# An expert with a single chunk of rows gets an arm of its own for its first product, with the rows stationary

## The chip, the cores and the metric

The kernel runs on one core of a Trainium2 chip. The metric is the device time of one execution in microseconds (us), taken from outside the profile; before the change its median over three runs is 671.97 us.

## The reference, cut to what matters

Three stages follow one another: local attention, a mixture of eight experts (each token goes to one of them), and a Fourier mixer with a channel MLP. The change lies in the second.

```python
def _moe_ref(x, w_gate, w_local, w1, w2):          # x 2 x 768 x 512, w1 8 x 512 x 1024, w2 8 x 1024 x 512
    logits = np.einsum('bsd,de->bse', x, w_gate)
    local_gate = 1.0 / (1.0 + np.exp(-np.einsum('bsd,de->bse', x, w_local).squeeze(-1)))
    for b in range(B):
        prev_e = -1
        for s in range(S):
            fresh_e = int(np.argmax(logits[b, s]))
            e = fresh_e if s == 0 or local_gate[b, s] < 0.5 else prev_e     # prev_e >= 0
            prev_e = e
            ...
            h = np.maximum(x[b, s] @ w1[e], 0.0)
            out[b, s] = p[e] * (h @ w2[e])
def reference(...):
    x = attention(q, k, v)
    x = _moe_ref(x, **moe)
    return _moe2_ref(x, **moe2)                    # FFT mixer, layer norm, channel MLP
```

How many tokens an expert has depends on the data. With the inputs of these runs experts 0 to 7 have 324, 177, 166, 172, 115, 206, 96 and 280 tokens.

## The kernel before

Routing writes for each expert a list of its tokens. `Moe.expert(e, n, more)` then works through one expert in chunks of 128 rows; `n` is its number of chunks, held in registers and known only at run time. Experts 0 to 6 take one path of the code and expert 7 (`LAST`) another. In expert 0 the first chunk has been dealt with earlier, so its chunks here are 1 and 2 (`at = 1`); in the others they are 0 and 1 (`at = 0`).

**First product.** `first256` (L1160) always multiplies two chunks, 256 rows, with blocks of w1 stationary: four groups of 24 matmuls of 128x256, since float32 accuracy is made of three matmuls (weight and row each split in a high and a low part). After each group ScalarE takes the relu into `hh` (L1163), and VectorE the low part `hl` (L1164). A chunk that has no tokens is multiplied all the same. **Third chunk.** `third()` follows in a branch (L1226). **Second product.** `second` (L1140) multiplies the first chunk into `y` with 24 matmuls of 128x512; a branch (L1249) does the same for the second chunk, into `more`. An engine that does not take a branch jumps over it.

`first128` (L1190) is the other form of the first product, for 128 rows: the rows are stationary, and w1 streams past in two halves of 12 matmuls of 128x512. Its result lies the wrong way round for the second product, so ScalarE copies each half out of PSUM into `hs` (L1195), TensorE transposes it in four matmuls (L1179), and relu and low part follow (L1181, L1182). The third chunk and expert 7 use it.

**What runs beside it.** `ring.take` yields small steps, and `step` places two of them between the groups of matmuls; all engines run their instructions in the order in which they were emitted. The steps cast the next expert's weights: ScalarE rounds a piece of 128x1024 to the high part (L1006), and VectorE subtracts for the low part (L1008). Eight units of kind "d" go between them: pieces of a mixing matrix, stored as words of two halves, that are decoded here and used after the experts. Such a unit is an absolute value on ScalarE (L1019), four steps on VectorE (L1028, L1030, L1032, L1034) and a store to HBM on GpSimd's queue (L974). Experts 0 and 3 have two d units, one during each product, expert 6 has none, and the others have one during the first product. Their tiles, named `dec`, come from a pool of two buffers, which `hs` in `first128` shares. `tokens(e + 1)` places the transposes of the next expert's two chunks (L1102, in PSUM tiles `xtp` of a pool of two) between the matmuls of `y`, and ScalarE and VectorE take their two parts (L1105, L1106). On GpSimd's queue stand also the gathers of rows (L1070) and the scatters of results (L1127).

The framework counts the semaphores. Behind a branch, a wait is set so that it holds whichever arm was taken; the shorter arm adds what it lacks to the counts.

Of the kernel before, what the change touches and what calls it, by code (L numbers as in the profile page):

```python
# [23 lines left out]
P = 128  # L24
# [12 lines left out]
LAST = E - 1  # L37
# [850 lines left out]
def rows(st, g):  # L888

    n = 2 if g % 4 < 2 else 4  # L890
    out = []
    for j in range(2):
        hi, lo = (t.rearrange("p (k n) -> p k n", k=n) for t in st.ring.get("e", g + j))
        out += [(hi[:, k], lo[:, k]) for k in range(n)]
    return out
# [142 lines left out]
class Moe:  # L1038
# [79 lines left out]
    def write(self, y, p, d, name="more", beside=None):  # L1118

        nc = self.tc.nc  # L1120
        ys = self.work.tile([P, DM], F32, name=name, bufs=2 if name == "ys" else 1)
        nc.scalar.activation(ys, y, AF.Copy, scale=p)
        self.scatter(ys, d, beside)
# [74 lines left out]
    def expert(self, e, n, more):  # L1198
        tc, ring = self.tc, self.st.ring
        pc, ent = self.pc[e % 2], self.ent[e % 3]  # L1200
        w1, w2 = rows(self.st, 4 * e), rows(self.st, 4 * e + 2)
        bg = Background()

        def chain(*gs):
            for g in gs:
                yield from g


        at = 0 if e else 1
        step = lambda: bg.step(2)  # L1210
        spare = self.ps_more, "more"

        def result(c, h, y, ys, *more):
            y = self.second(*h, w2, *y, *more)
            bg.drain()
            last = e == LAST and c == 1
            write = lambda: self.write(y, pc[:, c:c + 1], ent[:, c, 1:2], ys, "first" if last else None)
            if last:
                self.finish = write
            else:  # L1220
                write()

        def third():
            self.weight(e, (2,))

            with tc.If(n > 2):  # L1226
                for _ in self.turn(2, 0, self.place(e, 2)):
                    pass
                if e == LAST:
                    self.rest(more)  # L1230
                late = self.first128(w1, *self.more, spare, spare)
                result(2, self.more[1], spare, "more", lambda: None, late)

        first, then = ([ring.take(*u, follow=e < LAST) for u in units] for units in ring.plan[e])
        if e < LAST:
            bg.add(chain(*first))
            self.gathers(e + 1)
            if e + 2 < E:
                self.entries(e + 2)
            calls = iter(range(8))  # L1240
            self.first256(e, lambda: bg.step(2) if e or next(calls) > 1 else None)
            bg.drain()
            if e:
                third()
            bg.add(self.tokens(e + 1))
            bg.add(chain(*then))
            own = lambda c: [t[0][:, :, c * P:(c + 1) * P] for t in (self.hh, self.hl)]
            result(at, own(0), (self.ps_y, "y"), "ys", step)
            with tc.If(n > at + 1):  # L1249
                result(at + 1, own(1), spare, "more")  # L1250
            return

        for c in range(2):
            x, h = ([t[:, :, c * P:(c + 1) * P] for t in s] for s in ((self.xh[e % 2], self.xl[e % 2]), (self.hh[0], self.hl[0])))
            late = self.first128(w1, x, h, (self.ps_h, "h"), (self.ps_x, "xtp"), step, [x[:, :DM] for x in self.xg[:2]])
            if c == 0:
                third()
                bg.add(chain(*first))
            result(c, h, (self.ps_y, "y"), "ys", step, late)
            if c == 0:  # L1260
                self.fetch(0)
# [562 lines left out]
```

## Time and profile before

| | us |
|---|---|
| median of 3 runs (lowest, highest) | 671.97 (671.45, 672.93) |
| the profiled execution | 671.14 |
| its span, and what lies outside it | 669.4 and 1.74 |
| busy in the span: TensorE, VectorE, ScalarE, GpSimd | 643.4, 391.7, 272.1, 68.5 |
| experts 0 to 6, first to last matmul (146.18 to 301.59) | 155.4 |

The engines are named PE (TensorE matmul), PEld (its weight load), DVE (VectorE), ACT (ScalarE), POOL (GpSimd) and SP (SyncE, which issues loads). A name such as ACTq is the engine's own sequencer. [...] A matmul's listed duration overlaps with the next one's: how long a row of them takes is read from the starts. Idle time ahead of an instruction stands in brackets with what ended it. L12 is line 12 of the kernel.

### The profile page before, as it was taken

What the parts mean: (1) busy time and instruction counts of PE and PEld (TensorE: products, weight loads), DVE (VectorE), ACT (ScalarE), POOL (GpSimd) and SP (SyncE); (2) the same over time, 40 slices, a digit from 0 to 9 for tenths busy, and PEclk for the clock granted to TensorE, in tenths of its full rate; (3) what the DMA queues carried; (4) which work ended last, traced back from release to release, by engine and by line L of the source; (5) the groups of instructions that cost most, each with busy time, mean ns of one, the idle gap of its engine ahead of it and who ended that gap; (6) DMA issues with size and microseconds to landing.
All of it is one profiled execution on the core that took longest, in us unless ns stands there. A gap on an engine that the chain in (4) does not pass through costs nothing.

```text
span 669.4 us, 9817 instructions
## 1 busy us (share of the span) xinstructions
PE 643.4 (96%) x3606; PEld 530.6 (79%) x3607; DVE 391.7 (59%) x931; ACT 272.1 (41%) x478; POOL 68.5 (10%) x83
## 2 busy tenths in 40 slices
PE   9999998879999999999999999999999999999997
PEld 5888887559988998897857687877788888888885
DVE  4667777518968789762357977899451131254112
ACT  6657666118555756563423542542221121141110
POOL 0010112230331333120100000000000000000000
PEclk9999999779999999999988799999999999999999
DMA  8656433447998799763260133353010010100001
GB/s 303 249 182 145 110 128 103 142 133 280 330 378 298 245 336 343 289 253 139 68 265 18 64 126 126 125 190 125 1 64 0 1 63 1 64 0 1 0 1 63
DMA packets 26096, 96.21 MB, mean 144 GB/s; under 512 B 7764, under 2 KB 8916, under 8 KB 18096
## 3 DMA queue, kind: packets, MB, share of 16 engines
q1 hardware_dynamic: 20288, 81.19, 35.5%
q0 software_dynamic: 4736, 10.56, 4.4%
q10 hardware_dynamic: 1008, 3.65, 1.4%
q8 instruction: 35, 0.57, 0.4%
q14 instruction: 29, 0.24, 0.1%
HBM read 84.75 MB, written 14.88 MB: 149 GB/s over the span
## 4 chain that ended last, share of the span: by engine, by line
PE 42%; DVE 9%; ACT 2%; issue 1%; DVEq 0%; ACTq 0%
PE h L1634 17%; PE acc L1649 5%; PE acc L1650 5%; PE acc L1648 5%; DVE dec L1032 1%; DVE dec L1034 1%; PE acc L1455 1%; PE y L1140 1%; PE more L1190 1%; PE h L1190 1%; PE acc L1469 1%; PE more L1140 1%; DVE dec L1030 1%; PE f L1600 1%; DVE dec L1028 1%
## 5 line engine op out<-in xcount | busy, mean ns | idle before, releaser
L1639 DVE SCALAR_TENSOR_TENSOR hl<-h,hh 128x512 fp32r<-128x512 f32 x48 | 33.1, 689 | 120.4 <-ACT hh L1638 120.4
L1638 ACT ACTIVATE hh<-h 128x512 fp32r<-128x512 f32 x48 | 28.7, 597 | 156.4 <-PE h L1634 151.4
L1008 DVE TENSOR_TENSOR wide<-raws,wide 128x1024 fp32r<-128x1024 f32 (+2 forms) x46 | 50.4, 1110 | 26.1 <-ACT wide L1006 26.0
L174 ACT ACTIVATE t<-t,nm 128x256 f32<-128x256 f32 (+1 forms) x96 | 39.2, 479 | 29.4 <-DVE nm L166 29.4
L1006 ACT CAST wide<-raws 128x1024 fp32r<-128x1024 f32 (+2 forms) x46 | 43.1, 959 | 6.4 <-PE acc L1650 3.5
L197 PE MATMUL op<-vs,p 128*128 128x75 f32 x352 | 43.5, 277 | 2.1 <-PE tp L183 1.1
L197 PEld LDWEIGHTS op<-vs,p 128*128 128x128 f32 x352 | 42.1, 195 | 3.0 <-PE tp L183 2.0
L1634 PE MATMUL h<-un0h,wide 128*128 128x512 f32 (+1 forms) x136 | 42.8, 381 | 0.1
L166 DVE CUSTOM_DVE_ANT_0 t<-sp,bias 128x256 f32<-128x256 f32 (+1 forms) x96 | 32.8, 398 | 9.7 <-PE sp L157 7.3
L1649 PE MATMUL acc<-wide,hh 128*128 128x512 f32 x96 | 38.2, 398 | 0.0
L1648 PE MATMUL acc<-wide,hh 128*128 128x512 f32 x96 | 37.9, 394 | 0.0
L1650 PE MATMUL acc<-wide,hl 128*128 128x512 f32 x96 | 37.7, 393 | 0.0
L1634 PEld LDWEIGHTS h<-un0h,wide 128*128 128x128 f32 x136 | 25.0, 188 | 5.5 <-ACT un0h L1410 0.3
L1163 ACT ACTIVATE hh<-h 128x512 fp32r<-128x512 f32 x28 | 16.8, 599 | 30.2 <-PE h L1160 26.7
L1160 PE MATMUL h<-xh,wide 128*128 128x256 f32 x192 | 27.7, 280 | 0.1
L1070 POOL DMA_INDIRECT xg<-xs,ent x23 | 25.4, 1104 | 14.2 <-issue 6.7
L1634 PE MATMUL h<-un0l,wide 128*128 128x512 f32 (+1 forms) x68 | 25.9, 380 | 0.0
L183 PE MATMUL tp<-consts,t 128*128 128x128 f32 x176 | 25.3, 281 | 0.5 <-ACT p L189 0.4
L1164 DVE SCALAR_TENSOR_TENSOR hl<-h,hh 128x512 fp32r<-128x512 f32 x28 | 19.2, 685 | 10.8 <-ACT hh L1163 8.6
L1160 PEld LDWEIGHTS h<-xh,wide 128*128 128x128 f32 x192 | 24.9, 188 | 0.8 <-issue 0.5
L189 ACT COPY p<-tp 128x512 f32<-128x512 f32 (+1 forms) x48 | 25.1, 536 | 0.7 <-PE tp L183 0.6
L183 PEld LDWEIGHTS tp<-consts,t 128*128 128x128 f32 x176 | 19.3, 143 | 5.0 <-PE sp L157 1.0
(441 smaller groups left out, 1609.6 us busy)
## 6 DMA issues: line engine op xcount, KB each, us to landing
raws<-we SPq DMA_DIRECT2D x30, 1024.0 KB
raws<-wm SPq DMA_DIRECT2D x17, 1024.0 KB
raws<-wmf SPq DMA_DIRECT2D x7, 1024.0 KB
wmf<-dec POOLq DMA_DIRECT2D x8, 512.0 KB, 8.6
vs<-v SPq DMA_DIRECT2D x6, 600.0 KB
xs<-xrow SPq DMA_DIRECT2D x12, 260.0 KB
vt<-vT SPq DMA_DIRECT2D x6, 512.0 KB
raws<-kq SPq DMA_DIRECT2D x3, 1024.0 KB
```

Of the source, the lines that this page charges most:

```text
L166: V.tensor_tensor_reduce(out=u.t[:, x, :u.W], in0=u.sp[:, j, k, :u.W], in1=bias[:, 4 * u.g + x, u.b0:u.b0 + u.W], scale=-0.125, scalar=3.0 ...
L174: A.activation(u.t[:, x, :u.W], u.t[:, x, :u.W], AF.Exp, bias=u.nm[:, x:x + 1], scale=-1.0)
L183: T.transpose(u.tp[k][:, j, c], u.t[:, 2 * k + j, c * P:(c + 1) * P], st.ident)
L197: T.matmul(u.op[:, x], u.p[:, x, c], vs[:, ti % KS, u.h + x], start=c == 0, stop=c == len(tiles) - 1)
L1006: (first or nc.scalar.copy)(hi[:, cs], raw[:, cs])
L1008: (eng() if callable(eng) else eng or nc.vector).tensor_tensor(lo[:, cs], raw[:, cs], hi[:, cs].bitcast(F32), op=ALU.subtract)
L1160: T.matmul(ps[:, u], w[:, f], x[:, k], start=n == 0, stop=n == 11)
L1634: nc.tensor.matmul(ps[:, c], a[:, k], x[:, k, c], start=n == 0, stop=n == 11)
L1639: nc.vector.scalar_tensor_tensor(hl, ps, 0.0, hh.bitcast(F32), op0=ALU.max, op1=ALU.subtract)
L1648: T.matmul(acc[c], hh[:, cs], h2, start=first, stop=False)
L1649: T.matmul(acc[c], hh[:, cs], l2, start=False, stop=False)
L1650: T.matmul(acc[c], hl[:, cs], h2, start=False, stop=last)
```

## The change

For experts 0 to 6 the first product gets a branch on the expert's count. With more than one chunk the `If` arm holds what was there, `first256` with its background steps. With one chunk the `Else` arm runs `first128` on it, 24 matmuls of 128x512 and two groups of four transposes, with the same casts and decodes beside it. The gathers of the next expert and the entries of the one after it stay ahead of the branch. The lines behind the edit move down by 10: L1249 becomes L1259, and L1241 is the new branch.

```diff
-        first, then = ([ring.take(*u, follow=e < LAST) for u in units] for units in ring.plan[e])
+        takes = lambda n: [ring.take(*u, follow=e < LAST) for u in ring.plan[e][n]]
         if e < LAST:
-            bg.add(chain(*first))
             self.gathers(e + 1)
             if e + 2 < E:
                 self.entries(e + 2)
-            calls = iter(range(8))
-            self.first256(e, lambda: bg.step(2) if e or next(calls) > 1 else None)
-            bg.drain()
+            begun = dict(ring.begun)
+            s = e % 2
+            with tc.If(n > at + 1) as two:
+                bg.add(chain(*takes(0)))
+                calls = iter(range(8))
+                self.first256(e, lambda: bg.step(2) if e or next(calls) > 1 else None)
+                bg.drain()
+            with two.Else():
+
+                ring.begun = begun
+                bg.add(chain(*takes(0)))
+                x, h = ([t[:, :, :P] for t in ts] for ts in ((self.xh[s], self.xl[s]), (self.hh[0], self.hl[0])))
+                self.first128(w1, x, h, (self.ps_h, "h"), (self.ps_x, "xtp"), step)()
+                bg.drain()
             if e:
                 third()
             bg.add(self.tokens(e + 1))
-            bg.add(chain(*then))
+            bg.add(chain(*takes(1)))
             own = lambda c: [t[0][:, :, c * P:(c + 1) * P] for t in (self.hh, self.hl)]
             result(at, own(0), (self.ps_y, "y"), "ys", step)
@@
             if c == 0:
                 third()
-                bg.add(chain(*first))
+                bg.add(chain(*takes(0)))
             result(c, h, (self.ps_y, "y"), "ys", step, late)
```

Three places show how instructions and waits move. The first is TensorE at the start of expert 0's second product, before:

```order
L1140 MATMUL y_6533<-wide_103,hh256_6304 128x512 x2
L1102 MATMUL xtp_6537<-consts_66,xg0_6328 128x128 [waits DMASW0_49]
L1102 MATMUL xtp_6537<-consts_66,xg0_6328 128x128 x3
L1140 MATMUL y_6533<-wide_103,hh256_6304 128x512
L1140 MATMUL y_6533<-wide_103,hh256_6304 128x512 [waits Activation_49]
L1140 MATMUL y_6533<-wide_103,hh256_6304 128x512
L1102 MATMUL xtp_6549<-consts_66,xg1_6329 128x128 [waits DMASW1_49]
L1102 MATMUL xtp_6549<-consts_66,xg1_6329 128x128 x3
```

And after:

```order
L1140 MATMUL y_6605<-wide_103,hh256_6304 128x512 x2
L1102 MATMUL xtp_6609<-consts_66,xg0_6328 128x128 [waits DMASW0_49,DVE_49,PE_49]
L1102 MATMUL xtp_6609<-consts_66,xg0_6328 128x128 x3
L1140 MATMUL y_6605<-wide_103,hh256_6304 128x512 x3
L1102 MATMUL xtp_6621<-consts_66,xg1_6329 128x128 [waits DMASW1_49,DVE_49,PE_49]
L1102 MATMUL xtp_6621<-consts_66,xg1_6329 128x128 x3
```

Each of the two transposes of tokens waited for its gather alone; now they wait for VectorE too, since the `Else` arm uses the two `xtp` tiles: the first for the ninth VectorE instruction of the `If` arm, the second for its last. All of experts 0 to 6 have this.

The second place is ScalarE in expert 4, from the start of the first product to its end, before:

```order
L1006 CAST wide_103<-raws_63 128x1024 [waits DMAHW2_49,PE_49]
L1163 ACTIVATE hh256_6304<-h_7691 128x512 [waits DVE_49,PE_49]
L1006 CAST wide_103<-raws_63 128x1024
L1006 CAST wide_103<-raws_63 128x1024 [waits DMAHW3_49]
L1163 ACTIVATE hh256_6304<-h_7722 128x512 [waits DVE_49,PE_49]
L1006 CAST wide_103<-raws_63 128x1024
L1019 ACTIVATE dec_7780<-raws_63 128x1024 [waits DMAHW4_49,DMASW0_49,DVE_49]
L1163 ACTIVATE hh256_6304<-h_7754 128x512 [waits PE_49]
L1163 ACTIVATE hh256_6304<-h_7788 128x512 [waits DVE_49,PE_49]
```

And the `Else` arm, which takes its place for one chunk:

```order
L1006 CAST wide_103<-raws_63 128x1024 [waits DMAHW2_49,PE_49]
L1006 CAST wide_103<-raws_63 128x1024 [waits PE_49]
L1006 CAST wide_103<-raws_63 128x1024 [waits DMAHW3_49,PE_49]
L1006 CAST wide_103<-raws_63 128x1024 [waits PE_49]
L1195 COPY dec_8156<-h_8157 128x512 [waits PE_49,Activation_49]
L1019 ACTIVATE dec_8185<-raws_63 128x1024 [waits DMAHW4_49,DMASW2_49,DVE_49]
L1181 ACTIVATE hh256_6304<-xtp_8192 128x4x128 [waits PE_49]
L1195 COPY dec_8156<-h_8180 128x512 [waits PE_49]
L1181 ACTIVATE hh256_6304<-xtp_8210 128x4x128 [waits PE_49]
```

Four casts now stand ahead of the first copy of a half, and the absolute value of the d unit (L1019) stands between the two copies. It waits for DMASW2, which here is the store of expert 3's second d unit; before, it waited for DMASW0, the store of expert 3's first. TensorE's two groups of transposes in that arm each wait for the copy of their half:

```order
L1190 MATMUL h_8180<-sl5h_6295,xh0_6322 128x512
L1190 MATMUL h_8180<-sl5l_6296,xh0_6322 128x512
L1179 MATMUL xtp_8192<-consts_66,dec_8156 128x128 [waits Activation_49]
L1179 MATMUL xtp_8192<-consts_66,dec_8156 128x128 x3
L1190 MATMUL h_8180<-sl5h_6295,xh0_6322 128x512
L1190 MATMUL h_8180<-sl5l_6296,xh0_6322 128x512
L1190 MATMUL h_8180<-wide_103,xl0_6325 128x512 x2
L1190 MATMUL h_8180<-sl5h_6295,xl0_6325 128x512 x2
L1179 MATMUL xtp_8210<-consts_66,dec_8156 128x128 [waits DVE_49,Activation_49]
L1179 MATMUL xtp_8210<-consts_66,dec_8156 128x128 x3
```

The third place is ScalarE at the end of expert 3's second product, before:

```order
L1006 CAST sl1h_101<-raws_63 128x1024
L1019 ACTIVATE dec_7608<-raws_63 128x1024 [waits DMAHW1_49,DMASW1_49,Activation_49]
L1122 ACTIVATE ys_7625<-y_7566,pc1_6309 128x512 [waits DMASW4_49,DVE_49,PE_49]
L1249 REGISTER_ALU x2
L1249 COMPARE_AND_BRANCH
```

And after:

```order
L1006 CAST sl1h_101<-raws_63 128x1024
L1019 ACTIVATE dec_7926<-raws_63 128x1024 [waits DMASW0_49,DMAHW1_49,DVE_49,Activation_49]
L1122 ACTIVATE ys_7943<-y_7884,pc1_6309 128x512 [waits DMASW4_49,PE_49]
L1259 REGISTER_ALU x2
L1259 COMPARE_AND_BRANCH
```

Expert 3's second absolute value waited for DMASW1, the store of expert 2's d unit. It now waits for DMASW0, the store of expert 3's own first. In expert 0 the second absolute value likewise waits for the store of the first.

## Rows read from the trace of the kernel before

**Rows 1.** Windows of two experts: stretch, length, busy time (instructions) by engine, PEclk, DMA share, GB/s

```profile
241.50:259.79 18.29, 17.99 (x129) 16.40 (x128) 15.63 (x21) 12.99 (x17) 6.56 (x7) 1.00 0.88 295
283.00:301.59 18.59, 18.29 (x131) 16.63 (x130) 12.04 (x16) 11.81 (x16) 4.56 (x4) 1.00 0.68 262
```

**Rows 2.** Timeline of TensorE, experts 4 and 6: start, duration, engine, line, operation, count

```profile
241.50 0.63 PE L1160 MATMUL h<-xh,wide 128*128 128x256 f32 x4
...
252.47 0.39 PE L1160 MATMUL h<-xl,sl5h 128*128 128x256 f32 x2
253.01 0.47 PE L1140 MATMUL y<-sl0h,hh 128*128 128x512 f32 x1
...
294.81 0.93 PE L1140 MATMUL y<-wide,hh 128*128 128x512 f32 x3
```

**Rows 3.** Timeline of TensorE, expert 7, which uses the other form

```profile
301.59 1.16 PE L1190 MATMUL h<-wide,xh 128*128 128x512 f32 x4
...
305.85 0.60 PE L1179 MATMUL xtp<-consts,xg 128*128 128x128 f32 x4
306.21 0.48 PE L1190 MATMUL h<-sl5h,xh 128*128 128x512 f32 x1
```

**Rows 4.** Timeline of ScalarE, expert 7: the copy of a half

```profile
304.65 0.59 ACT L1195 COPY xg<-h 128x512 f32<-128x512 f32 x1 [2.49 <-PE h L1190]
```

**Rows 5.** Timeline of TensorE: the end of the jump over the unused half of the attention

```profile
139.25 1.02 PE L50 MATMUL more<-busy 128*128 128x512 bf16 x4 [1.07 <-issue]
```

**Rows 6.** Timeline of TensorE, then VectorE, in expert 0: second tokens; last step of the decode

```profile
161.25 0.60 PE L1102 MATMUL xtp<-consts,xg 128*128 128x128 f32 x4
162.71 1.23 DVE L1034 SCALAR_TENSOR_TENSOR dec<-raws,dec 128x1024 int32<-128x1024 int32 x1
```

**Rows 7.** Timelines: second tokens and last low part in expert 3, then in expert 5

```profile
231.49 0.60 PE L1102 MATMUL xtp<-consts,xg 128*128 128x128 f32 x4
231.01 0.69 DVE L1164 SCALAR_TENSOR_TENSOR hl<-h,hh 128x512 fp32r<-128x512 f32 x1
273.29 0.60 PE L1102 MATMUL xtp<-consts,xg 128*128 128x128 f32 x4
273.81 0.68 DVE L1164 SCALAR_TENSOR_TENSOR hl<-h,hh 128x512 fp32r<-128x512 f32 x1
```

**Rows 8.** Timeline of GpSimd: expert 3's two stores; landing of all eight, then the second

```profile
231.39 0.58 POOL L974 DMA_DIRECT2D wmf<-dec  x1 [6.61 <-DVE dec L1034]
...
242.01 0.56 POOL L974 DMA_DIRECT2D wmf<-dec  x1 [10.03 <-DVE dec L1034]
DMA to landing us min/median/max: 7.0/8.6/10.0
DMA to landing us min/median/max: 7.8/7.8/7.8
```

**Rows 9.** Timelines of ScalarE, then VectorE: experts 3 and 4, d unit and casts

```profile
234.99 1.16 ACT L1019 ACTIVATE dec<-raws 128x1024 f32<-128x1024 f32 x1
...
242.33 1.04 ACT L1006 CAST wide<-raws 128x1024 fp32r<-128x1024 f32 x1
...
244.99 1.99 ACT L1006 CAST wide<-raws 128x1024 fp32r<-128x1024 f32 x2
237.78 0.69 DVE L1028 TENSOR_SCALAR dec<-dec 128x1024 f32<-128x1024 f32 x1
...
240.49 1.22 DVE L1034 SCALAR_TENSOR_TENSOR dec<-raws,dec 128x1024 int32<-128x1024 int32 x1
```

**Rows 10.** Timeline of TensorE at two gaps, each with the window that follows (columns as in 1)

```profile
143.49 2.02 PE L1102 MATMUL xtp<-consts,xg 128*128 128x128 f32 x8 [3.21 <-issue]
143.60:150.10 6.50, 5.83 (x26) 5.21 (x27) 1.50 (x4) 1.17 (x2) 2.03 (x2) 0.50 0.64 232
370.22 0.44 PE L1455 MATMUL acc<-wide,sl0l 128*128 128x386 f32 x1 [1.54 <-DVE sl0l L1411]
372.50:378.50 6.00, 6.00 (x19) 4.21 (x19) 5.66 (x22) 1.06 (x2) 0.00 (x0) 0.50 0.12 16
```

## The prediction

> **What bounds the kernel now.** I read the windows of the experts first. From the first matmul of expert 4 to that of expert 5 lie 18.29 us, in which TensorE is busy for 17.99, at the full clock; expert 6 takes 18.59 with 18.29 busy [rows 1]. No other engine reaches 16 us there. So TensorE paces this stage, and a microsecond taken from or added to its row of instructions comes out at the end, as long as the others keep up. A window does not show how near the others are to not keeping up. For that I read the timelines, and the order of the changed program, for each wait that is new.
>
> **What the edit is meant to take away.** In expert 4 the 96 matmuls of the first product, one jump and the start of the second product take 253.01 - 241.50 = 11.51 us [rows 2]; in expert 6 294.81 - 283.00 = 11.81. Expert 7 runs the other form: 18 matmuls of 128x512 take 305.85 - 301.59 = 4.26, so 0.237 each, and four transposes 0.36 [rows 3]. A whole arm is then 24 x 0.237 + 2 x 0.36 = 6.4 us on TensorE. With two jumps the second product could start 7.0 us in, 4.5 to 4.8 us earlier, in two experts (4 and 6, with 115 and 96 tokens). That gross gain of some 9 us is not what I forecast, since the halves have to go through ScalarE, and since the new arm changes waits in all seven experts.
>
> **Jumps.** The one jump over an arm not taken that is in the first rows costs TensorE 253.01 - (252.47 + 2 x 0.117) = 0.31 [rows 2], where 0.117 is 11.2 us over 96 matmuls (11.51 less the jump). Each expert now makes one more. The far jump over the attention's unused half cost at most 1.07 [rows 5]. The new arms are small, so I take 0.31; the end of the range is 1.07, or 0.76 more for each jump.
>
> **Expert 0: +2.7.** The second transposes of tokens stood at 161.25. They now wait for the last VectorE instruction of the first product, which here is the last step of a d unit, ending at 162.71 + 1.23 = 163.94 [rows 6]. Queued behind them on TensorE is the rest of the second product. The jump lies within this wait: +2.7. The second absolute value here now waits for the store of the first d unit, issued 0.3 behind that same step, landing 7.0 to 10.0 later [rows 8]. Behind it on ScalarE stands only the result's scaling, behind its decode on VectorE a cast for expert 2 and then expert 1's first low part. I take 0, as the tokens' wait has already moved TensorE by 2.7; up to 3.0 if the store needs 10.0 instead of 7.0.
>
> **Experts 1, 2 and 3: +0.9.** The same wait is there for the last low part, which in expert 3 ends at 231.70, against transposes at 231.49 [rows 7]: 0.2, within the jump's 0.31. Expert 3 stands for the three: 3 x 0.3.
>
> **Expert 4: +4.75.** This is the large term, and its cause begins in expert 3. There the second absolute value, at 234.99 before [rows 9], now waits for expert 3's first store, issued at 231.39 and landing 8.6 later (the median) at 240.0 [rows 8]. It ends at 241.2; two scalings of 0.6 follow, and the casts of expert 4 begin at 242.35, where they did (242.33). But the decode on VectorE, which takes 240.49 + 1.22 - 237.78 = 3.93 [rows 9], now ends at 245.1 instead of 241.7. The second store goes out 0.3 later, at 245.4, and with its 7.8 [rows 8] lands at 253.2, which is 11.7 after expert 4's start. All further times count from there. GpSimd's scatters and the gathers for expert 5 stand behind that store and move with it, but their rows are wanted only at 15.
>
> ScalarE: the casts start at 0.85; four at 0.97 (two took 1.99, [rows 9]) end at 4.75, and the copy of the first half (0.59, [rows 4]) at 5.3. TensorE, with its 18 matmuls done at 0.31 + 4.26 = 4.6, waits until then, transposes to 5.7, and ends its last six matmuls at 7.1. Next in ScalarE's row is the absolute value, held for the store until 11.7. It ends at 12.9, the relu at 13.45, the copy of the second half at 14.0. TensorE stands still from 7.1 to 14.0, transposes until 14.35, jumps, and begins the second product at 14.65, against 11.51: +3.15. VectorE then owes two short steps of the decode (0.7 each), a low part (0.6), two long steps (1.25 each) and the last low part: 18.05. The second tokens would come six matmuls and four transposes behind 14.65, at 16.45, and wait 1.6 for it. Sum 3.15 + 1.6 = 4.75. With both stores at 7.0 the same working gives +2.3, with both at 10.0 +8.3.
>
> [...]
>
> **Expert 5: +0.75.** The last low part ends at 274.49, the transposes stood at 273.29 [rows 7]: +1.2. ScalarE's part of it may shrink, since expert 4 gives its loads more time; then the jump's 0.3 is left. I take the middle.
>
> **Expert 6: -3.4.** There is no d unit, so nothing stands between the two copies. Casts until 4.75 and the first copy until 5.3 as above, transposes to 5.7, six matmuls to 7.1, second copy to 7.7, transposes to 8.05, jump: 8.4 against 11.81. The last low part is done at about 9.3, ahead of the tokens.
>
> **The clock: +1.6.** [...] Expert 4's gap is 6.9 long. Half the clock for 6.4 us costs 3.2, of which the 1.6 that the tokens wait anyway are hidden. Bounds 0 and 3.2.
>
> **Sum.** 2.7 + 0.9 + 4.75 + 0.75 - 3.4 + 1.6 = +7.3. The profiled execution took 671.14 (span 669.4, 1.74 around it), so 678.4; the median of the runs is 0.83 higher than it: 679.3.
>
> **Rivals.**
> A, faster: the waits cost nothing, because stores land before they are asked for and VectorE is done in time. Then expert 0 to 3 and 5 pay a jump each (+1.55), and expert 4 gains like expert 6 (-3.4): 1.55 - 6.8 = -5.2, 666.7. It decides at a landing below 234.99 - 231.39 = 3.6 us, and needs the token wait to be no wait. Every landing listed speaks against it (7.0 at least), and so does the 163.94 of expert 0.
> B, no change: only the stores are fast. Expert 4 then starts its second product at 8.4 but its decode delays the tokens by 1.6, so -1.6; with 2.7 + 0.9 + 0.3 - 3.4 the sum is -1.1, 670.9.
> C, a second fall of the clock: expert 0's gap is at most 2.4 long (163.94 less 161.25 and a jump), if it falls in one piece. After 1.54 idle the clock was 0.50 for 6.0 us in a later stretch, which was lightly loaded before [rows 10]; here TensorE had been fully busy. If it falls, up to 3.2 more: 682.5.
> D, long jumps: 0.76 more in experts 0 to 3, 5 and 6 less what the waits hide (expert 0's): 5 x 0.76 = +3.8, 683.1.
> E, the arm is not taken: neither expert has one chunk. Then waits alone are left, 2.7 + 6 x 0.3 = +4.5, 676.5. The token counts speak against it.
>
> **How the numbers follow.** Forecast (with its own spread of +2.3 to +8.3 in expert 4) 0.55, C 0.17, D 0.10, E 0.03, A 0.08, B 0.07. The forecast's own range is 675 to 683; with C and D on one side, and B and A left out, the range is 674.5 to 685.5. A measurement of this kernel can tell about 0.2% from no change, 1.3 us. B stands for "same" with 0.07, A for "faster" with 0.08, the rest is slower: 0.85.
>
> **What would show it.** In the changed profile: no L1160 in experts 4 and 6, and L1190 in their place (else E); in expert 0, L1102 a second time at about 164 with VectorE as releaser; L1019 in expert 3 and expert 4 idle until a store lands; a gap of some 7 us on TensorE in expert 4 between L1190 and the second group of L1179, and 0.50 in the clock behind it; second product of expert 6 at 8.4 after its start. I am wrong if L1019 starts at once in expert 4 (B), if tokens do not wait (A), or if expert 4 loses over 8.3 (a store or a load that I have not seen).

## The result, and the profile after

The changed kernel takes 679.54 us (median of 20 runs, 673.11 to 685.6), against 672.39 for the kernel before in its 20 runs. The ratio, from which disturbed executions are left out, is 1.0094, with a 95% interval of 1.0075 to 1.0113: slower by about 0.9%, or 6.3 us. The span of the profiled execution is 676.6 us, against 669.4.

The windows of the changed kernel that answer to [rows 1], for expert 0, expert 4 and expert 6, each from its first matmul to the next expert's (columns as there; PEclk is the clock granted to TensorE, as a share of its full speed):

```profile
147.36:176.44 29.08, 26.59 (x152) 23.74 (x153) 19.17 (x26) 13.84 (x17) 3.62 (x4) 0.88 0.87 319
...
247.84:269.06 21.22, 15.24 (x65) 11.41 (x64) 16.75 (x21) 13.28 (x17) 7.29 (x7) 0.92 0.84 282
...
292.93:310.23 17.30, 13.87 (x65) 10.21 (x64) 11.48 (x15) 11.80 (x16) 5.52 (x4) 1.00 0.72 256
```

Experts 4 and 6 have 65 matmuls listed instead of some 130, so the new arm runs. TensorE has 2.8 us less to do in expert 4 than before, and expert 4 is 2.9 us longer: 6.0 of its 21.2 us are idle. Expert 6 has 4.1 less to do and is only 1.0 shorter (the window of expert 6 in [rows 1] begins 0.3 us early; from the first matmul at 283.30 TensorE was busy for 17.99).

The timeline of TensorE in expert 0 shows the second product and the two transposes of tokens, as in [rows 6]:

```profile
160.30 0.86 PE L1140 MATMUL y<-wide,hh 128*128 128x512 f32 x3
161.99 0.63 PE L1102 MATMUL xtp<-consts,xg 128*128 128x128 f32 x4 [0.83 <-issue]
...
164.98 1.08 PE L1102 MATMUL xtp<-consts,xg 128*128 128x128 f32 x4 [1.66 <-issue]
```

VectorE's last step of the decode starts at 163.66 there, takes 1.23, and the second transposes follow it:

```profile
163.66 1.23 DVE L1034 SCALAR_TENSOR_TENSOR dec<-raws,dec 128x1024 int32<-128x1024 int32 x1
```

They take 1.08, where the first took 0.63. The window from their start shows why, PEclk 0.50:

```profile
164.90:166.00 1.10, 1.02 (x5) 1.05 (x6) 1.10 (x2) 0.00 (x0) 0.58 (x1) 0.50 0.31 30
```

For experts 3 and 4 the timelines of GpSimd, ScalarE and TensorE belong together; they answer to [rows 8], [rows 9] and [rows 2]:

```profile
237.41 0.59 POOL L974 DMA_DIRECT2D wmf<-dec  x1 [6.62 <-DVE dec L1034]
249.93 0.56 POOL L974 DMA_DIRECT2D wmf<-dec  x1 [11.93 <-DVE dec L1034]
```

```profile
244.54 1.12 ACT L1019 ACTIVATE dec<-raws 128x1024 f32<-128x1024 f32 x1 [3.44 <-DMA wmf<-dec]
...
248.67 3.88 ACT L1006 CAST wide<-raws 128x1024 fp32r<-128x1024 f32 x4
252.46 0.57 ACT L1195 COPY dec<-h 128x512 f32<-128x512 f32 x1
257.32 1.12 ACT L1019 ACTIVATE dec<-raws 128x1024 f32<-128x1024 f32 x1 [4.29 <-issue]
```

```profile
253.09 0.66 PE L1179 MATMUL xtp<-consts,dec 128*128 128x128 f32 x4 [0.89 <-ACT dec L1195]
...
259.46 0.66 PE L1179 MATMUL xtp<-consts,dec 128*128 128x128 f32 x4 [4.32 <-ACT dec L1195]
260.26 0.76 PE L1140 MATMUL y<-sl0h,hh 128*128 128x512 f32 x1
...
263.73 0.60 PE L1102 MATMUL xtp<-consts,xg 128*128 128x128 f32 x4
```

This is the chain of the prediction. The first store goes out at 237.41, and the absolute value starts 7.1 us later. The second goes out at 249.93, and expert 4's absolute value starts 7.4 later. ScalarE stands between its two copies for 4.29 us and TensorE between its two groups of transposes for 4.32. The second product starts 12.42 us into expert 4 (11.51 before). For expert 4's absolute value the profile names no releaser ("issue"); that it is the store there too is shown by e2_rot below, in which that wait is gone.

In expert 6 the second product starts at 8.77 us instead of 11.51. Of these 2.74 us, 1.74 are lost at the second tokens, whose gather has not landed (they stand 12.41 us after the start, and 8.77 + 1.90 = 10.67 would have been possible):

```profile
301.70 0.94 PE L1140 MATMUL y<-wide,hh 128*128 128x512 f32 x3
...
305.34 0.63 PE L1102 MATMUL xtp<-consts,xg 128*128 128x128 f32 x4 [1.57 <-DMA xg<-xs,ent]
```

### The profile page after: what moved, and what is told of

Same layout as the page of the kernel before. It is cut to its first block, busy times and chain, and to the rows that moved or that the text cites. A ratio compares the mean times of both kernels' runs of the same rounds, so it can differ in the third digit from the quotient of the medians.

```text
span 676.6 us, 9698 instructions
## 1 busy us (share of the span) xinstructions
PE 638.1 (94%) x3478; PEld 520.2 (77%) x3479; DVE 389.3 (58%) x927; ACT 272.2 (40%) x478; POOL 69.7 (10%) x83
## 4 chain that ended last, share of the span: by engine, by line
PE 41%; DVE 9%; ACT 2%; issue 1%; DVEq 0%; ACTq 0%
PE h L1644 16%; PE acc L1659 5%; PE acc L1660 5%; PE acc L1658 5%; DVE dec L1032 1%; DVE dec L1034 1%; PE y L1140 1%; PE acc L1479 1%; PE acc L1465 1%; PE more L1190 1%; PE h L1190 1%; PE more L1140 1%; DVE dec L1030 1%; PE f L1610 1%; DVE dec L1028 1%
## 5 line engine op out<-in xcount | busy, mean ns | idle before, releaser
L1649 DVE SCALAR_TENSOR_TENSOR hl<-h,hh 128x512 fp32r<-128x512 f32 x48 | 33.0, 688 | 120.4 <-ACT hh L1648 120.4
L1648 ACT ACTIVATE hh<-h 128x512 fp32r<-128x512 f32 x48 | 28.7, 597 | 156.4 <-PE h L1644 151.4
L1070 POOL DMA_INDIRECT xg<-xs,ent x23 | 26.9, 1170 | 15.6 <-issue 6.8
L1019 ACT ACTIVATE dec<-raws 128x1024 f32<-128x1024 f32 x18 | 20.6, 1142 | 15.6 <-issue 9.4
L1160 PE MATMUL h<-xh,wide 128*128 128x256 f32 x160 | 22.7, 280 | 0.6 <-PEq L1259 0.6
L1034 DVE SCALAR_TENSOR_TENSOR dec<-raws,dec 128x1024 int32<-128x1024 int32 x18 | 22.1, 1225 | 0.6
L1644 PE MATMUL h<-un1h,wide 128*128 128x512 f32 x64 | 21.7, 400 | 0.7 <-ACT un1h L1420 0.7
```

The lines of the kernel that those rows point to most:

```text
L1034: V.scalar_tensor_tensor(t, lo, 29, t, op0=ALU.logical_shift_right, op1=ALU.bitwise_or)
L1644: nc.tensor.matmul(ps[:, c], a[:, k], x[:, k, c], start=n == 0, stop=n == 11)
L1649: nc.vector.scalar_tensor_tensor(hl, ps, 0.0, hh.bitcast(F32), op0=ALU.max, op1=ALU.subtract)
```

## The experiments

Each was run beside the kernel before, on the same chip as it. The table gives the lengths in us from the first matmul of an expert to that of the next, from the timelines of TensorE, the sum over experts 0 to 6, and the measured ratio to before. Without a stall expert 0 varies between 24.4 and 25.9 from one profile to another, as TensorE runs slower in the first part of it, for longer or shorter: PEclk is 0.50 for its first 4.1 us in the kernel before, and the matmuls of 128x256 start 0.21 us apart, instead of 0.12 behind that, for the first 2.8 us in e13_six_ent and the first 6.0 in e14_six_late; differences under 1.5 us in that column say nothing.

| kernel | 0 | 1 | 2 + 3 | 4 | 5 | 6 | sum | ratio (95% interval) |
|---|---|---|---|---|---|---|---|---|
| before | 25.05 | 23.43 | 46.84 | 18.29 | 23.51 | 18.29 | 155.41 | 1 |
| the change | 29.08 | 23.90 | 47.50 | 21.22 | 23.87 | 17.30 | 162.87 | 1.0094 (1.0075, 1.0113) |
| e1_never | 28.31 | 27.02 | 47.51 | 19.12 | 25.05 | 18.29 | 165.30 | 1.0109 (1.0075, 1.0143) |
| e2_rot | 28.27 | 23.75 | 47.49 | 16.86 | 25.94 | 15.62 | 157.93 | 1.0024 (0.9994, 1.0053) |
| e3_ps | 25.39 | 26.73 | 46.85 | 21.43 | 23.50 | 16.65 | 160.55 | 1.0075 (1.0046, 1.0105) |
| e4_both | 24.76 | 24.06 | 46.84 | 20.72 | 23.58 | 17.65 | 157.61 | 1.0022 (0.9996, 1.0048) |
| e5_no0 | 25.55 | 23.81 | 47.50 | 22.50 | 23.85 | 16.78 | 159.99 | 1.0049 (1.0014, 1.0084) |
| e8_six | 24.58 | 23.42 | 46.84 | 18.29 | 24.33 | 16.75 | 154.21 | 0.9973 (0.9955, 0.9992) |
| e9_free | 24.56 | 23.97 | 46.85 | 17.42 | 25.22 | 15.61 | 153.63 | 0.9979 (0.9953, 1.0006) |
| e10_free_q | 24.51 | 23.99 | 46.85 | 17.21 | 25.26 | 16.02 | 153.84 | 0.9963 (0.9937, 0.9989) |
| e11_free_ent | 25.32 | 32.03 | 46.83 | 24.24 | 23.50 | 15.60 | 167.52 | 1.0171 (1.0141, 1.0201) |
| e12_before_ent | 25.84 | 32.36 | 46.85 | 21.35 | 23.49 | 18.29 | 168.18 | 1.0163 (1.0118, 1.0208) |
| e13_six_ent | 24.43 | 31.58 | 46.80 | 18.81 | 23.50 | 15.60 | 160.72 | 1.0080 (1.0049, 1.0110) |
| e14_six_late | 25.87 | 23.42 | 46.84 | 18.29 | 24.07 | 15.66 | 154.15 | 0.9948 (0.9920, 0.9977) |

**The arm in the program, never taken (e1_never).**

```diff
-            with tc.If(n > at + 1) as two:
+            with tc.If(n > 0) as two:
```

> The new arm stands in the program, but its condition is changed so that no expert takes it: all of experts 0 to 6 run the old arm. Theory W (waits that the arm brings to everybody): expert 0 still loses its 4.0 us (tokens wait for VectorE, and the clock falls behind that), each of the other six pays a jump of 0.3, in all +5.8 us on the kernel before (ratio 1.0086, 1.006 to 1.010). Rival L (the loss is made inside the new arm, by its copies and transposes): only jumps are left, 7 x 0.31 = +2.2 us (1.003).

Measured 1.0109. The mere presence of the arm costs as much as the change, so the rival that lays the loss on the arm's own work falls. My own 5.8 us were too few: expert 1 takes 3.6 more, where I had put 0.3, and experts 4 and 5 together 2.4. At the end of expert 0 its second absolute value waits, by the order of the program for a store, as ScalarE's timeline shows, and with it the gathers of expert 2 come late in expert 1 (TensorE's timeline):

```profile
175.67 1.12 ACT L1019 ACTIVATE dec<-raws 128x1024 f32<-128x1024 f32 x1 [5.57 <-issue]
```

```profile
191.22 1.02 PE L1102 MATMUL xtp<-consts,xg 128*128 128x128 f32 x4 [1.03 <-DMA xg<-xs,ent]
```

**The two kinds of waits taken apart (e2_rot, e3_ps, e4_both).** In e2_rot the copied halves lie in the tile of the third chunk's rows, unused when there is one chunk, and both arms share one `dec` tile for a d unit:

```diff
-        t = self.work.tile([P, PW // 2], F32, name="dec")
+        t = self.pre.pop(r, None) if r in self.pre else self.work.tile([P, PW // 2], F32, name="dec")
@@
+            ds = [ring.at[u] for u in ring.plan[e][0] if u[0] == "d" and ring.at[u] not in begun]
+            held = {r: ring.work.tile([P, PW // 2], F32, name="dec") for r in ds}
+            ring.pre = dict(held)
@@
-                ring.begun = begun
+                ring.begun, ring.pre = begun, dict(held)
@@
-                self.first128(w1, x, h, (self.ps_h, "h"), (self.ps_x, "xtp"), step)()
+                own_hs = [self.xg[2 + e % 2][:, :DM]] * 2
+                self.first128(w1, x, h, (self.ps_h, "h"), (self.ps_x, "xtp"), step, own_hs)()
```

> The changed kernel with the store waits taken away: the copied halves go into an unused tile of gathered rows instead of the pool of decoded pieces, and both arms share one tile for a decoded piece, so that the buffers rotate as before the change. The tokens' wait for VectorE stays. Theory W: expert 4's second absolute value and copy start at once, expert 4 goes from +2.9 to about -1.6 (the second product 3 us earlier, the tokens 1.6 late), no clock fall there; expert 0 keeps +4.0, expert 6 its -1.3: +2.8 us on before (1.004, 1.002 to 1.006), 4.5 below the change. Rival L (ScalarE's order, not the store): nothing changes, +6 to +7 (1.009).

In e3_ps only the PSUM tiles of the transposes change:

```diff
-                self.first128(w1, x, h, (self.ps_h, "h"), (self.ps_x, "xtp"), step)()
+                self.first128(w1, x, h, (self.ps_h, "h"), spare, step)()
```

> The changed kernel with the transposes of the new arm in PSUM tiles of the other pool (that of the third and second chunks), so that the tokens wait for their gather alone as before. The store waits stay. Theory W: expert 0 goes from +4.0 to +0.3 and no half clock follows there; experts 1 to 3 and 5 pay a jump, expert 4 keeps about +2.5 and expert 6 -1.3: +2.7 us on before (1.004, 1.002 to 1.006). Rival L: no change against the changed kernel, 1.009.

e4_both has both edits.

> Both cures together: halves in an unused tile of gathered rows, one tile for a decoded piece in both arms, transposes in the other PSUM pool. Theory W: what is left is a jump in five experts (+1.5), and the gain of the arm in experts 4 and 6, -3.3 and -1.3 to -3.4 each: -3 to -5 us on before (ratio 0.992 to 0.996), faster than both. Rival L (the arm itself does not pay): no faster than before, 1.000 or above.

Each cure does in its own place what it should. With the store waits gone (e2_rot), expert 4 falls from 21.22 to 16.86 us, and expert 0 stays at 28.27. With the token waits gone (e3_ps), expert 0 falls to 25.39, experts 2 and 3 to what they were before, and expert 4 stays at 21.43. The totals follow the forecasts only in part. The 1.0024 of e2_rot lies within its range (1.002 to 1.006), though expert 5 is 2.4 longer and expert 6 shorter than that forecast had them; 1.0075 for e3_ps (range 1.002 to 1.006) and 1.0022 for both (0.992 to 0.996) lie outside. Three things are behind that.

First, the two waits cover each other in expert 0. When the tokens no longer wait, expert 0's store is late in relation to TensorE, and the 3 us come back in expert 1 of e3_ps, first on ScalarE, then on TensorE:

```profile
171.92 1.13 ACT L1019 ACTIVATE dec<-raws 128x1024 f32<-128x1024 f32 x1 [6.16 <-DMA wmf<-dec]
```

```profile
178.82 0.73 PE L1160 MATMUL h<-xh,wide 128*128 128x256 f32 x4 [1.00 <-DVE hl L1164]
...
187.64 0.63 PE L1102 MATMUL xtp<-consts,xg 128*128 128x128 f32 x4 [1.28 <-DMA xg<-xs,ent]
```

Experts 0 and 1 together take 48.48 before, 52.98 after the change, 52.02 and 52.12 with one cure, and 48.82 with both.

Second, in e2_rot an expert 4 that is 1.4 shorter than before is followed by an expert 5 that is 2.4 longer, as its casts wait for weights, and TensorE then for VectorE:

```profile
267.67 1.05 ACT L1006 CAST sl0h<-raws 128x1024 fp32r<-128x1024 f32 x1 [2.52 <-DMA raws<-we]
```

```profile
270.63 1.21 PE L1160 MATMUL h<-xh,wide 128*128 128x256 f32 x8 [0.84 <-DVE hl L1164]
```

Third, in e4_both expert 3's second absolute value still waits (4.66 us, until 242.01), for a store: the buffers rotate in another order there than in e2_rot, and the wait is gone in e9_free below, which takes the third chunk's halves out of that pool. It holds nothing in expert 4 but the store on GpSimd's queue, and the gathers behind that store. The tokens then wait 2.83 for theirs, and expert 4 takes 20.72:

```profile
256.37 0.63 PE L1102 MATMUL xtp<-consts,xg 128*128 128x128 f32 x4 [2.83 <-DMA xg<-xs,ent]
```

**Expert 0 without the branch (e5_no0).** The new lines of the edit; behind its `else` stands the branch as in the change.

```diff
+            if e == 0:
+                bg.add(chain(*takes(0)))
+                calls = iter(range(8))
+                self.first256(e, lambda: bg.step(2) if next(calls) > 1 else None)
+                bg.drain()
+            else:
```

> The changed kernel with the branch left out of expert 0, which keeps the old first product for any count; experts 1 to 6 as changed. Theory W: expert 0's 4.0 us (2.55 of waiting tokens, 1.5 of slower clock) and the 0.5 in expert 1 go, the rest stays (experts 2, 3: 0.3 each, expert 4 +2.9, expert 5 +0.6, expert 6 -1.3): +2.9 us on before, 1.004 (1.002 to 1.006). Rival (the stall only moves on to the next expert's first branch): 1.009 as the change.

Measured 1.0049: expert 0 is back at 25.55, and its stall does not move on to expert 1 (23.81), so the rival falls. Expert 4 is 1.3 longer than in the change; its gap is 4.77 instead of 4.32, and its second product starts at 13.35.

**The arm in expert 6 alone (e8_six).** `if e < LAST - 1:` keeps the old first product; expert 6 has the branch, with the halves in the unused tile and the transposes in the other pool, as in e4_both.

> Only expert 6 has the branch, with the copied halves in an unused tile of gathered rows and the transposes in the other PSUM pool, so that nothing else moves. Theory W: expert 6 alone saves 2.7 us (as in the run with the store waits taken away), less up to 1.7 if the second tokens' gather is late: -1.0 to -2.7 on before, 0.996 to 0.9985. Rival (the arm does not pay even here): 1.000.

0.9973, as expected: expert 6 takes 16.75 instead of 18.29. So the arm itself does pay. Its second tokens wait 0.95 for the gather.

**All new waits gone (e9_free), and less traffic (e10_free_q).** e9_free is e4_both with the third chunk's halves out of the `dec` pool too:

```diff
-                late = self.first128(w1, *self.more, spare, spare)
+                late = self.first128(w1, *self.more, spare, spare, lambda: None, None if e == LAST else [self.xg[2 + e % 2][:, :DM]] * 2)
```

> All new waits taken away: both cures, and the third chunk's copied halves out of the pool of decoded pieces too, so that no absolute value waits for a store younger than before. Theory D (what is left is bounded by the loads of weights): expert 4 gets 2.7 us shorter, expert 5 about 2.4 longer, as its casts wait for their loads, and expert 6 saves 1.0 to 2.7: -1 to -3 us on before, 0.9955 to 0.9985. Rival (the waits were all): experts 4 and 6 save 2.7 each, expert 5 stays at 23.5: -5.4 us, 0.992.

e10_free_q loads only a quarter of each d unit and leaves the other three quarters out.

```diff
-            (queue or nc.sync).dma_start(t.bitcast(I32), io["wm"][n].bitcast(I32))
+            (queue or nc.sync).dma_start(t[:, :PW // 4].bitcast(I32), io["wm"][n][:, :PW // 8].bitcast(I32))
```

> The same kernel, but of each d unit only a quarter is loaded, 0.25 instead of 1 MB (the rest of the piece holds old data): 6 MB less traffic over experts 0 to 5, of which 3 MB in experts 3 to 5. Theory D: expert 5's casts no longer wait for their loads, expert 4 stays at 15.6 and expert 5 comes down to 23.5: 2 to 2.5 us less than the run above, 0.992 to 0.995 of before. Rival (something other than the traffic makes expert 5 longer): no difference to the run above.

The windows of experts 4 and 5, first of e8_six, in which expert 4 does not have the arm, then of e9_free, in which it does:

```profile
242.08:260.37 18.29, 18.00 (x129) 16.39 (x128) 14.84 (x20) 11.61 (x15) 6.57 (x7) 1.00 0.82 260
260.37:284.70 24.33, 23.72 (x152) 21.30 (x153) 19.14 (x23) 14.62 (x19) 6.93 (x6) 1.00 0.84 327
```

```profile
246.23:263.65 17.42, 13.87 (x65) 10.22 (x64) 13.44 (x18) 11.40 (x15) 7.94 (x7) 1.00 0.84 263
263.65:288.87 25.22, 23.73 (x153) 21.32 (x153) 19.14 (x23) 14.75 (x19) 7.49 (x6) 1.00 0.90 354
```

The sums are 42.62 and 42.64 (41.80 before). TensorE has 4.1 us less to do in expert 4, and experts 4 and 5 together are not shorter. Part of the gain is lost within expert 4, where the tokens wait for their gather, and the rest in expert 5:

```profile
257.15 0.63 PE L1102 MATMUL xtp<-consts,xg 128*128 128x128 f32 x4 [1.15 <-DMA xg<-xs,ent]
```

What the lengths of e9_free gain is expert 6's alone, and its ratio, 0.9979, is not clear of 1. That the d units' traffic bounds expert 5 falls with e10_free_q: with three quarters of their bytes gone, expert 5 takes 25.26 (25.22 with them), and the same cast waits 2.26 (2.33) for its weights. The other loads remain; the DMA share in expert 5 is 0.86 instead of 0.90.

**The queue that the weight loads stand in (e11_free_ent, e12_before_ent, e13_six_ent).** SyncE's timeline shows the loads of expert 5's weights in a row behind the load of list entries, in the kernel before and in e9_free:

```profile
250.88 0.38 SPq L1086 DMA_DIRECT2D ent<-list  x1
251.37 2.08 SPq L946 DMA_DIRECT2D raws<-we  x2
```

```profile
256.58 0.38 SPq L1086 DMA_DIRECT2D ent<-list  x1
257.42 1.28 SPq L946 DMA_DIRECT2D raws<-we  x3
```

The entries' load waits for the scatters that still read that tile, 8.2 us in the kernel before, as the waits of SyncE's queue show, and the weights behind it leave 9.9 and 11.2 us after expert 4's start:

```profile
SPq L1086 <- DMA x<-more,ent: 8.2, 1, 8.2
```

Three kernels issue it behind the first product instead: e9_free, the kernel before, and e8_six, each with this edit.

```diff
-            if e + 2 < E:
-                self.entries(e + 2)
@@
+            if e + 2 < E:
+                self.entries(e + 2)
             bg.add(self.tokens(e + 1))
```

> The run with all new waits taken away, and one line moved: the load of the list entries for the expert after next (L1086) is issued behind the first product instead of ahead of it. On SyncE's queue it stands ahead of the weight loads and waits for the last scatter of the expert before. Theory Q (the queue): the loads of expert 5's weights leave 4 to 7 us earlier in expert 4, expert 5's casts do not wait, expert 5 falls from 25.2 to about 23.5, the rest stays: 1.7 us less than that run, 0.9955 of before (0.993 to 0.998). Rival D (the traffic, or the pool of raw pieces): the loads leave no earlier or land no earlier, 0.998.

> The kernel before with that line moved and nothing else. Theory Q: TensorE did not wait for weights in the profiled execution of the kernel before (expert 5 23.5 us), so the loads come earlier and nothing follows: 1.000 (0.998 to 1.001); it would win only in executions in which expert 5 is held as in the run with the arm in expert 6 alone (24.3). Rival D: no earlier loads, 1.000 too.

> The branch in expert 6 alone, with that line moved. Theory Q: expert 5 goes from 24.3 to 23.5, expert 6 stays at 15.6 to 16.8: 0.8 us less than without the move, 0.996 of before (0.994 to 0.998). Rival D: as without the move, 0.997.

For expert 5 the queue is shown by e13_six_ent against e8_six. The three loads of weights, in e8_six and then in e13_six_ent:

```profile
252.96 2.51 SPq L946 DMA_DIRECT2D raws<-we  x3
```

```profile
250.78 9.31 SPq L946 DMA_DIRECT2D raws<-we  x3
```

They leave 0.3 us after expert 4's start (250.49) instead of 10.9 (242.08), no cast of expert 5 waits for its load, and expert 5 takes 23.50 instead of 24.33, behind an expert 4 that is 0.5 longer. The other two kernels show less: e11_free_ent has 23.50 too, but behind an expert 4 that is 6.8 longer, which gives the loads time, and the 23.49 of e12_before_ent is what the kernel before had. The totals went the other way, by 0.8 to 1.7%, and no expectation had that. In e12_before_ent TensorE waits 5.92 us in expert 1 for the tokens of expert 2:

```profile
191.41 1.11 PE L1102 MATMUL xtp<-consts,xg 128*128 128x128 f32 x4 [5.92 <-DMA xg<-xs,ent]
```

Their gathers were issued as far into expert 1 as before (7.0 us after its start both times), but the one whose landing the trace lists took 11.2 us (10.9 in e11_free_ent), where the three before took 3.1 to 4.6 (the lines on L1070 in that stretch, of before and of e12_before_ent, each with the window of 178 to 186):

```profile
DMA to landing us min/median/max: 3.1/3.5/4.6
```

```profile
178.00:186.00 8.00, 7.85 (x58) 7.17 (x57) 7.79 (x12) 5.37 (x8) 3.90 (x4) 1.00 0.79 255
```

```profile
DMA to landing us min/median/max: 11.2/11.2/11.2
```

```profile
178.00:186.00 8.00, 7.34 (x58) 6.68 (x57) 7.93 (x10) 5.04 (x7) 5.03 (x4) 1.00 0.96 356
```

The weight loads now run beside the gathers: four leave between 175.5 and 186.5, where before one left at 173.71 and three from 182.89 on. The wait of the entries, which looked like an accident, had kept them apart. That it is the loads that slow the gathers is read from these rows; no run moves the loads alone.

**The tokens of expert 7 later (e14_six_late).** e8_six with

```diff
-            bg.add(self.tokens(e + 1))
+            bg.add(chain(iter(range(6 if e == LAST - 1 else 0)), self.tokens(e + 1)))
```

> The run with the branch in expert 6 alone, and the transposes of expert 7's tokens nine matmuls later in expert 6's second product. Theory G (what was left in expert 6 is the landing of expert 7's gathers, issued at a time that the arm does not move): no wait of the transposes, expert 6 takes 15.6 instead of 16.75 us, 1.1 less in all; with expert 5 between 23.5 and 24.3 that is -1.9 to -2.7 on before, ratio 0.996 to 0.997. Rival (expert 6 is held by something else): expert 6 stays at 16.75, 0.9973 as without the move.

Expert 6 takes 15.66 us and its tokens wait for nothing. The ratio is 0.9948 (0.9920 to 0.9977), somewhat below the expected 0.996 to 0.997, and faster than both kernels; what it shows over e8_six is read from expert 6's 1.1 us, since the two intervals overlap.

## Why the prediction was right, and where it was not

Forecast 679.3, measured 679.54. The direction and the mechanism hold: the arm changes the waits of all experts and loses more there than it saves. But that the sum came out so well is luck, because errors of both signs met in it. (By the ratio the loss is 6.3 us, by the two profiled spans 7.2, where I had 7.3.) The terms, with the lengths of the table:

| term | predicted | measured |
|---|---|---|
| expert 0 | +2.7 | +4.0 |
| experts 1 to 3 | +0.9 | +1.1 |
| expert 4, with the clock's 1.6 | +6.35 | +2.9 |
| expert 5 | +0.75 | +0.4 |
| expert 6 | -3.4 | -1.0 |
| sum | +7.3 | +7.5 |

**Expert 0.** The step was right: the second tokens stand 17.62 us after the start instead of 15.07, +2.55 for the 2.7. Counted from the start of the second product, the wait is 2.84 (4.68 us instead of 1.84), and 0.29 came back because the half clock at the expert's start ended sooner (0.50 for its first 3.6 us instead of 4.1); both groups of tokens wait, 0.83 and 1.66, where I had named the second alone. What was mis-sized is the clock, which I had left to rival C. From the tokens to the end of the expert it took 11.46 us instead of 9.98: +1.5, with the clock at 0.50 from 164.6 to 168.0. That rival's size (up to 3.2) was too large, and its place was right. The stretch that I called lightly loaded there was so only at its end: TensorE was busy for 8.58 of the 10.20 us ahead of that gap (360.00 to 370.20). Nor does the gap alone decide it: in e1_never and e2_rot the gaps ahead of the tokens are the same 0.83 and 1.66 us, and that stretch takes 10.0. The store's wait at the end of expert 0, put at 0 up to 3.0 "as the tokens' wait has already moved TensorE", was right in the change (expert 1 +0.5), and e3_ps shows the 3.0: it takes 3.3 when the tokens do not wait.

**Experts 1 to 3.** The sum was about right, and its step was wrong. I charged a jump of 0.31. In e4_both, where each of them makes two jumps, the second product of expert 2 starts at 11.51 as before: the second jump costs nothing that TensorE's row shows; what the 0.31 ahead of the second product is made of, no run isolates. The 0.3 come from what I had held to be inside the jump, the tokens that wait for the last low part: at 13.69 instead of 13.41 in expert 2, and at 13.42 again once that wait is gone.

**Expert 4.** The chain was right up to the start of the second product, and two links were mis-sized. The stores landed in 7.1 and 7.4 us, where I had taken 8.6 and 7.8, so TensorE's gap was 4.3 instead of 6.9 and the second product started at 12.42 instead of 14.65. With the landings as measured, my working gives 4.75 - 1.9 = 2.85, and the measured 2.9 leaves nothing for the clock's 1.6 on top. For the clock I had put 6.4 us at half, a length that [rows 10] show behind another gap and that no run shows here; it did fall, to 0.50 for 3.4 us, from 260.2 to 263.6:

```profile
261.50:263.50 2.00, 2.00 (x8) 1.51 (x6) 1.97 (x4) 1.20 (x3) 0.31 (x1) 0.50 1.00 422
```

The second tokens stood 3.47 us after the start of the second product instead of 1.90, and these 1.57 look like the 1.6 that I had predicted as a wait for the last low part. But TensorE does not wait there: it is busy for all of that window, at half the clock, and the low part ends at 263.49, ahead of the tokens at 263.73:

```profile
262.81 0.68 DVE L1182 SCALAR_TENSOR_TENSOR hl<-xtp,hh 128x512 fp32r<-128x512 f32 x1
```

The wait and the slow clock cover the same stretch, and I had added up two terms of which only one is paid. That the wait exists shows e2_rot, whose mean granted clock is 0.977 (0.970 in the change): there the second tokens stand 2.74 us after the start of the second product (0.36 of it for the first tokens' gather), right behind a low part that ends at 258.58. What is left of expert 4's 2.9, behind 0.91 and 1.57, is 0.45. It stands at the end of the expert, where the first matmul of expert 5 waits for TensorE's own sequencer at a branch, which the kernel before does not list; why, no run shows:

```profile
269.06 1.20 PE L1160 MATMUL h<-xh,wide 128*128 128x256 f32 x8 [0.62 <-PEq L1259]
```

Rival B falls with 7.1 and 7.4 us, as no store was fast.

**Expert 5.** Within the two ends that I gave (0.3 and 1.2), nearer to the lower.

**Expert 6.** This is the step that failed. "The last low part is done at about 9.3, ahead of the tokens" looked at VectorE and not at the gather. The tokens stood at 12.41 instead of 10.7, waiting for rows whose gather goes out behind a scatter on GpSimd's queue at a time that the arm does not move: the first of the three gathers starts 2.5 us after expert 6's first matmul in both kernels. e14_six_late shows it: with the tokens nine matmuls later expert 6 takes 15.66. Another 0.3 was the start, which I took from the window's edge at 283.00, while the first matmul listed stands at 283.30.

**What the prediction did not see at all** is that the gain in expert 4 is worth nothing even with every new wait gone (e8_six against e9_free): the tokens wait for a gather that does not come sooner, and expert 5's weights leave when SyncE's queue lets them. Whether a version exists in which they leave earlier and the gathers still land in time stays open; it was not tried.

## What to carry to other kernels

A new arm of a branch can be paid by everyone who passes it: in this framework, tiles that it takes from a shared pool, in SBUF or PSUM, put waits behind the branch for the arm that was not taken too (1.0109 in e1_never, where no expert takes it), so give a rare arm tiles of its own, and put the branch only where it can win. Two waits at the same place can hide each other, and one removed alone gains little (experts 0 and 1 took 52.98 us with both, 52.02 and 52.12 with one, 48.82 with neither). And ask whether what the next stage needs (loads, gathers) is released by the work that got faster: here it was not, and with 4.1 us less for TensorE in expert 4 the two experts took 42.64 us instead of 42.62.

## What the runs showed of the hardware that I had not expected

A second jump right behind the first added nothing to TensorE's row in expert 2 (11.51 us to the second product with one in the kernel before and with two in e4_both). A gather that shared the DMA engines with loads of 1024 KB each took 11.2 us (10.9 in a second kernel) instead of 3.1 to 4.6 to land, at a DMA share of 0.96 instead of 0.79 in the same stretch. And of three kernels with gaps of 0.83 and 1.66 us on TensorE, the change had 0.50 of the clock behind them, and 11.46 us from the second tokens to the end of the expert; the other two took 10.0 there.
